# A second layer in seven products of half the width, for the last wide chunk of the second MLP

## The chip, the core and the metric

The kernel runs on one NeuronCore of a Trainium2 chip. The metric is device time in microseconds (us) of one execution; a smaller one is better. TensorE (PE in the profile) multiplies, with weight loads (PEld) beside it; VectorE (DVE), ScalarE (ACT) and GpSimd (POOL) work element by element; DMA transfers are issued from the queue of SyncE (SP). TensorE writes to PSUM, which VectorE and ScalarE read and GpSimd doesn't; everything else lies in SBUF.

## The reference

Four sequences of 576 tokens pass through windowed attention with 8 heads of 64, then through two MLP blocks. What the change touches is the last of them:

```python
def _moe2_ref(x, g_ln, w_ch1, w_ch2):
    mu = np.mean(x, axis=-1, keepdims=True)
    var = np.mean((x - mu) ** 2, axis=-1, keepdims=True)
    xn = (x - mu) / np.sqrt(var + 1e-06) * g_ln
    ch = np.maximum(xn @ w_ch1, 0.0) @ w_ch2
    return (x + ch).astype(np.float32)
```

`x` has 2304 rows (tokens) of 512, `w_ch1` is 512x2048 and `w_ch2` 2048x512. The first MLP block is of the same form with 1536 features.

## The kernel before

The 2304 tokens are 18 tiles of 128; the residual stream is 18 buffers `u[i]` of 128x512. Each operand of a product in the MLPs is split into a rounded high part and a low remainder (`xh`, `xl`, `w1h`, `w1l`, `hh`, `hl`, `w2h`, `w2l`), and a product is three matmuls: high by high, high by low, low by high. The high part is an ACT copy (L361) or a ReLU (L924), the low one a subtraction on DVE or POOL (L374, or L926 for the ReLU).

An MLP runs over three chunks of tokens: a wide one of 8 tiles (0 to 7), a small one of 2 (16, 17), a wide one of 8 (8 to 15). A chunk runs in steps; a step takes 256 features, of which the second MLP has eight. In a wide chunk the first layer of a step (`seven_products`, L977) already is Strassen's scheme in Winograd's form: sums of four quadrants of the tokens' inputs (`prep_wide`) and sums of weights (`w1_of`, tiles `st`) make seven products of 512 columns, six matmuls each, in place of eight. It leaves four blocks `hid[j, half]`: features `j` (0, 1) of 128, tokens of the first or last four tiles (`half`). A block is a ReLU on ACT (`hh`) and one on DVE that subtracts `hh` (`hl`). `keep` holds two PSUM banks into which sums are copied and accumulated upon.

The second layer (`second`, L1036) isn't in that scheme. For each of the 8 token tiles it runs six matmuls of 512 columns (2 feature blocks by 3) into one of two PSUM banks `acc`, whose lines are

```python
nc.tensor.matmul(o.t, hh.t[:, c:c + P], wh.t, start=j == 0, stop=False)
nc.tensor.matmul(o.t, hh.t[:, c:c + P], wl.t, start=False, stop=False)
nc.tensor.matmul(o.t, hl.t[:, c:c + P], wh.t, start=False, stop=j == 1)
```

(L1048 to L1050), and DVE adds the bank to `u[i]` (L1053). In the last step of the last MLP each `u[i]` then goes out by DMA. So a step of a wide chunk has 42 matmuls in the first layer and 48 in the second, all of 512 columns. `w2_of` makes and splits the two tiles of `w_ch2` in the first chunk, stores both parts to DRAM and loads them back in the later chunks.

The second layer of step s stands in the program between the parts of the first layer of step s + 1 (two, three and three tiles after each part). That order isn't the one in which it runs: `Plan` collects every operation with its buffers, gives each a due time from the TensorE work ahead of it, and sets the order of all engines by a list schedule with costs per engine. An operation that names several engines goes to the one that the plan finds best. Buffers are rings with fixed counts: `st`, which takes temporaries of 128x512, has six; `acc` two; `hh` and `hl` six each. A buffer of a ring is used again when every reader of its tenant is done, a DMA store among them.

## Time and profile before

| | |
|---|---|
| median of three runs | 854.18 us (853.12 to 854.47) |
| span of the profiled execution | 854.5 us |
| PE busy | 830.8 us, 97% of the span |
| DVE busy | 638.1 us, 75% |
| ACT, POOL busy | 394.3 us, 338.5 us |

The profiled execution's only own time is its span, which lies 0.3 us over the median of the runs. Sums below are made against the span. The attention fills about the first 170 us, the first MLP reaches to about 480 us, the second MLP's first wide chunk to about 620 us, its small one to about 675 us, and its last wide chunk to the end. TensorE's granted clock is 1.00 (2.4 GHz) in every stretch of 20 us from 200 to 840 us.

### The profile page before, as it was taken

The page shows a single profiled execution, that of the slowest core. Times are in us where ns is not written, and L with a number is a line of the kernel's source. Part 1 is how long each engine was busy: PE and PEld are TensorE (multiplying, and loading weights), DVE is VectorE, ACT ScalarE, POOL GpSimd, SP SyncE. Part 2 cuts the span into 40 slices and gives each one's busy share as a digit, 9 for nine tenths or more (in the row PEclk, how much of TensorE's full clock was granted, in tenths as well). Part 3 has the DMA queues.
Part 4 walks back from the last instruction along what each step waited for, and adds up shares of the span by engine and source line. Part 5 has one row for each costly group of instructions (what it writes and reads, how often), then busy time and mean ns, then how long its engine had stood idle before and what let it go on. Part 6 is the DMA issues. An engine that isn't in the chain of part 4 may idle for free.

```text
span 854.5 us, 13205 instructions
## 1 busy us (share of the span) xinstructions
PE 830.8 (97%) x4478; PEld 685.8 (80%) x4478; DVE 638.1 (75%) x1311; ACT 394.3 (46%) x952; POOL 338.5 (40%) x353
## 2 busy tenths in 40 slices
PE   7999999979999999999999999999999999999997
PEld 6777888758888887788887888788889888888885
DVE  5787777987887989987888956988676855555554
ACT  6888766643434535334357323336357422222220
POOL 2685445554433556532235524614234612221110
PEclk9999999999999999999999999999999999999999
DMA  8678736457677699978762521887477762221112
GB/s 296 187 207 265 242 103 213 146 179 241 200 234 240 228 324 337 348 252 268 264 210 74 178 92 48 264 263 258 154 259 234 247 198 74 74 75 49 50 50 98
DMA packets 73698, 164.96 MB, mean 193 GB/s; under 512 B 8352, under 2 KB 8480, under 8 KB 73632
## 3 DMA queue, kind: packets, MB, share of 16 engines
q1 hardware_dynamic: 73152, 162.83, 57.5%
q0 software_dynamic: 480, 1.31, 0.7%
q8 instruction: 35, 0.57, 0.3%
q14 instruction: 31, 0.25, 0.1%
HBM read 131.34 MB, written 31.46 MB: 191 GB/s over the span
## 4 chain that ended last, share of the span: by engine, by line
PE 83%; DVE 7%; ACT 4%; DMA 2%; issue 2%; POOL 1%; SPq 1%; ACTq 0%; DVEq 0%; POOLq 0%
PE acc L1048 12%; PE acc L1050 12%; PE acc L1049 12%; PE b L993 9%; PE b L995 9%; PE b L994 9%; PE ps_v L608 3%; PE ps_s L596 3%; PE p L848 1%; PE b L442 1%; PE b L441 1%; PE b L440 1%; PE ps_t L653 1%; DVE st L374 1%; PE tok L735 1%
## 5 line engine op out<-in xcount | busy, mean ns | idle before, releaser
L1053 DVE TENSOR_TENSOR u<-acc,u 128x512 f32<-128x512 f32 x252 | 172.9, 687 | 64.0 <-PE acc L1050 60.6
L1048 PE MATMUL acc<-w2h,hh 128*128 128x512 f32 x504 | 198.6, 394 | 5.3 <-DVE u L1053 4.7
L1050 PE MATMUL acc<-w2h,hl 128*128 128x512 f32 x504 | 196.6, 390 | 0.3 <-DVE hl L926 0.2
L1049 PE MATMUL acc<-w2l,hh 128*128 128x512 f32 x504 | 196.5, 390 | 0.0
L924 ACT ACTIVATE hh<-b 128x512 fp32r<-128x512 f32 (+1 forms) x140 | 74.5, 552 | 262.8 <-PE b L995 226.4
L993 PE MATMUL b<-xh,w1h 128*128 128x512 f32 x392 | 154.0, 393 | 3.6 <-DVE hl L926 3.4
L994 PE MATMUL b<-xl,w1h 128*128 128x512 f32 x392 | 153.3, 391 | 1.8 <-DVE xl L374 1.8
L995 PE MATMUL b<-xh,w1l 128*128 128x512 f32 x392 | 153.4, 391 | 0.2 <-DVE w1l L374 0.2
L926 DVE SCALAR_TENSOR_TENSOR hl<-b,hh 128x512 fp32r<-128x512 f32 (+1 forms) x140 | 85.8, 631 | 62.9 <-ACT hh L924 62.1
L374 POOL TENSOR_TENSOR w1l<-w,w1h 128x512 fp32r<-128x512 f32 (+1 forms) x53 | 67.6, 1275 | 134.0 <-ACT w1h L361 124.2
L1048 PEld LDWEIGHTS acc<-w2h,hh 128*128 128x128 f32 x504 | 94.7, 188 | 27.0 <-DVE u L1053 7.5
L1050 PEld LDWEIGHTS acc<-w2h,hl 128*128 128x128 f32 x504 | 94.6, 188 | 21.2 <-DVE hl L926 1.2
L1049 PEld LDWEIGHTS acc<-w2l,hh 128*128 128x128 f32 x504 | 94.7, 188 | 18.4
L374 POOL TENSOR_TENSOR w1l<-st,w1h 128x512 fp32r<-128x512 f32 x38 | 51.1, 1346 | 116.5 <-ACT w1h L361 103.2
L993 PEld LDWEIGHTS b<-xh,w1h 128*128 128x128 f32 x392 | 73.9, 189 | 19.8 <-DVE hl L926 3.8
L994 PEld LDWEIGHTS b<-xl,w1h 128*128 128x128 f32 x392 | 74.0, 189 | 17.4 <-DVE xl L374 2.3
L995 PEld LDWEIGHTS b<-xh,w1l 128*128 128x128 f32 x392 | 73.9, 189 | 16.1 <-DVE w1l L374 0.6
L416 ACT ACTIVATE e<-rh 128x512 bf16<-128x512 bf16 (+2 forms) x65 | 41.3, 635 | 74.0 <-DMA rh<-wb 33.6
L646 ACT ACTIVATE pr<-t,mn 128x128 f32<-128x128 f32 x144 | 55.9, 392 | 15.1 <-DVE mn L637 14.9
L663 POOL TENSOR_SCALAR_AFFINE_SELECT pf<-pf 128x512 f32<-128x512 f32 x64 | 42.3, 661 | 37.7 <-ACT pf L361 35.5
L374 DVE TENSOR_TENSOR b<-b,p 128x512 f32<-128x512 f32 x56 | 39.0, 697 | 23.6 <-PE b L995 23.1
L374 POOL TENSOR_TENSOR w2l<-w,w2h 128x512 fp32r<-128x512 f32 x23 | 32.1, 1395 | 46.1 <-ACT w2h L361 46.0
(118 smaller groups left out, 1369.3 us busy)
## 6 DMA issues: line engine op xcount, KB each, us to landing
w<-d SPq DMA_DIRECT2D x88, 256.0 KB, 4.6
rw<-wb SPq DMA_DIRECT2D x32, 512.0 KB, 4.5
rh<-wb SPq DMA_DIRECT2D x32, 512.0 KB, 4.7
rw<-wa SPq DMA_DIRECT2D x24, 512.0 KB, 4.5
rh<-wa SPq DMA_DIRECT2D x24, 512.0 KB, 4.5
d<-y SPq DMA_DIRECT2D x32, 256.0 KB, 4.4
keys<-kT SPq DMA_DIRECT2D x18, 256.0 KB, 4.3
q<-qT SPq DMA_DIRECT2D x18, 256.0 KB, 4.7
```

The source lines that it names most:

```text
L374: pl.op({e: cost[e] for e in on}, lambda e: ENGINE[e].tensor_tensor(get(), ga(), gb(), alu), [*several(a), *several(b), *also], several(dst))
L646: op({"ACT": 580}, lambda m=m: nc.scalar.activation(out=pr.t[:, m], in_=t.t[:, m], func=AF.Exp, bias=mn.t[:, m:m + 1], scale=-1.0, accum_o ...
L663: op({"POOL": 630}, lambda a=a: nc.gpsimd.affine_select(pf.t[:, a], pf.t[:, 1], [[0, 4], [1 - 2 * a, P]], (ALU.is_ge, ALU.is_gt)[a], 0.0, ...
L924: op({"ACT": act(n, True)}, lambda: nc.scalar.activation(out=hh.t[:, c], in_=go(), func=AF.Relu), [o], [(hh, key)])
L926: mark[0] = op({"DVE": dve(n)}, lambda: nc.vector.scalar_tensor_tensor(out=hl.t[:, c], in0=go(), scalar=0.0, in1=hh.t[:, c].bitcast(F32), ...
L993: nc.tensor.matmul(g.t, wh.t[:, w], xh.t, start=start and k == 0, stop=False, skip_group_check=True)
L994: nc.tensor.matmul(g.t, wh.t[:, w], xl.t, start=False, stop=False, skip_group_check=True)
L995: nc.tensor.matmul(g.t, wl.t[:, w], xh.t, start=False, stop=stop and k == 1, skip_group_check=True)
L1048: nc.tensor.matmul(o.t, hh.t[:, c:c + P], wh.t, start=j == 0, stop=False)
L1049: nc.tensor.matmul(o.t, hh.t[:, c:c + P], wl.t, start=False, stop=False)
L1050: nc.tensor.matmul(o.t, hl.t[:, c:c + P], wh.t, start=False, stop=j == 1)
L1053: op({"DVE": dve(DM)}, lambda o=o, i=i: nc.vector.tensor_tensor(u[i].t, o.t, u[i].t, ALU.add), [o], [u[i]])
```

## The change

In the last wide chunk of the second MLP (`FAST2`), the second layer too is done in seven products. The blocks are 2 feature blocks by 2 halves of the tokens by 2 halves of the output columns; a group `g` takes two tiles of each half, and there are two groups. A product is six matmuls of 256 columns, two tiles by three, so a step has 2 x 7 x 6 = 84 of them in place of 48 of 512.

- **Sums of features** (`parts_of`): `s1` to `s4`, made from the ReLU blocks by DVE, which takes one ReLU and one addition in one instruction (`relu_with`); blocks 00 and 11 are written a second time, unsplit, by ACT. `s1` to `s4` are then split, the high part on ACT, the low one on DVE or POOL.
- **Sums of weights** (`keep_sums`): made in the first wide chunk from the two tiles of `w_ch2`, four sums `t1` to `t4` of 128x256 in two `st` tiles, split with two more `st` tiles, and stored to DRAM (four DMAs of 256 KB per step). `sums_of` loads them in the last chunk (512 KB of high parts and 512 KB of low ones per step) into buffers that the conversion of weights used before.
- **Adding up** (`second_fast`): a group's banks are `a` and `c` (ring `acc`, two) and `b`, into which ACT copies `a` (`fork`) and on which matmuls then accumulate. Six additions of DVE per group go to `u`, each from a bank of two tiles by 256 columns, in place of four of 128x512. `TURNS` is the order in the program.
- The residual is one tile `u_all`, of which `u[i]` are slices, so that one addition reaches two tiles.
- `pe2` is the cost by which the plan counts a matmul of the new form.

```diff
+FAST2 = ((1, 2),)
+
+TURNS = [(0, 0), (1, 0), (2, 0), (5, 0), (3, 0), (0, 1), (6, 0), (1, 1), (4, 0), (2, 1), (5, 1), (3, 1), (6, 1), (4, 1)]
...
+def pe2(n):
+    return 13 + n / 2.4
...
-    u = [buf("big", [P, DM], F32, f"u{i}") for i in range(NTILE)]
+    u_all = buf("big", [P, NTILE, DM], F32, "u")
+    u = [Part(u_all, lambda t, i=i: t[:, i]) for i in range(NTILE)]
...
+        if any((layer, k) in FAST2 for k in range(c + 1, 3)) and c == 0:
+            keep_sums(layer, n, wtiles[used[0] - 2:used[0]], last)
+        return out if (layer, c) not in FAST2 else sums_of(layer, n, out)
+
+    def keep_sums(layer, n, w, last):
+
+        x0, x1 = w
+        temp = [buf("mlp", [P, DM], F32, "st", ST_BUFS) for _ in range(2)]
...
+        sub(0, x0, half(x0, 1), x0, half(x0, 0))
+        sub(1, x1, half(x1, 1), (temp[0], 0), t[0])
+        sub(2, x0, half(x0, 1), x1, half(x1, 1))
+        sub(3, x1, half(x1, 0), (temp[0], 1), t[1])
+        for k, y in enumerate(temp):
...
+            copy(h, lambda h=h: h.t.bitcast(F32R), y, lambda y=y: y.t, DM, ("ACT",))
+            minus(y, lambda y=y: y.t.bitcast(F32R), y, lambda y=y: y.t, h, lambda h=h: h.t, DM)
+            for p, z in (("h", h), ("l", y)):
+                op({"DMA": 728}, lambda k=k, p=p, z=z: nc.sync.dma_start(
+                    out=d[p].t[:, k * DM:(k + 1) * DM], in_=z.t), [z], [(d[p], k)], last)
...
+    def sums_of(layer, n, parts):
+
+        d = sums2[layer, n]
+        hi = buf("raw", [P, 2 * DM], F32R, "rw", 2)
...
+                op({"DMA": 1456 / len(xs)}, lambda p=p, k=k, x=x, w=w: nc.sync.dma_start(
+                    out=x.t.bitcast(F32), in_=d[p].t[:, k * w:(k + 1) * w]), [d[p]], [x])
...
+            if fast:
+                return parts_of(hid, j, half, g)
...
+    def parts_of(hid, j, half, g):
...
+        def split_h(x, h, k=None):
+            (hh, ghh), (hl, ghl) = inner(x, h, k)
+            t = temps[x]
+            split(hh, ghh, hl, ghl, t, lambda: t.t, CW, ("ACT",))
...
+        def relu_both(x, temporary):
+            h = hh, hl = hidden()
+            inner(x, h)
+            op({"ACT": act(CW, True)}, lambda: nc.scalar.activation(out=hh.t, in_=g.t, func=AF.Relu), [g], [hh])
...
+                op({"ACT": act(CW, True)}, lambda: nc.scalar.activation(out=t.t, in_=g.t, func=AF.Relu), [g], [t])
+            mark[0] = op({"DVE": dve(CW)}, lambda: nc.vector.scalar_tensor_tensor(
+                out=hl.t, in0=g.t, scalar=0.0, in1=hh.t.bitcast(F32), op0=ALU.max, op1=ALU.subtract), [g, hh], [hl])
...
+        def relu_with(x, y, alu):
+            t, z = temp(x), temps[y]
+            op({"DVE": dve(CW)}, lambda: nc.vector.scalar_tensor_tensor(
+                out=t.t, in0=g.t, scalar=0.0, in1=z.t, op0=ALU.max, op1=alu), [g, z], [t])
+            return t
+        if j == half:
+            relu_both("11" if j else "00", True)
+        elif half:
+            h = few()
+            s1 = relu_with("s1", "11", ALU.add)
+            relu_with("s3", "00", ALU.subtract)
+            s2, a = temp("s2"), temps["00"]
+            minus(s2, lambda: s2.t, s1, lambda: s1.t, a, lambda: a.t, CW)
+            split_h("s1", h, 0)
+            split_h("s3", h, 1)
+            split_h("s2", hidden())
+        else:
+            relu_both("01", False)
+            relu_with("s4", "s2", ALU.subtract)
+            split_h("s4", hidden())
...
+    def second_fast(s, w2, hid):
...
+        def bank_of(group, x):
+            if x not in group[3]:
+                group[3][x] = buf("psn", [P, 2, HW], F32, "acc", 2)
+            return group[3][x]
+
+        def product(group, x, h, w, start, stop):
...
+                for p in range(2):
+                    c = slice((2 * g + p) * P, (2 * g + p + 1) * P)
+                    for k, (x, y) in enumerate(((ghh, gwh), (ghh, gwl), (ghl, gwh))):
+                        nc.tensor.matmul(o.t[:, p], x()[:, c], y(), start=start and p == 0 and k == 0,
+                                         stop=stop and p == 1 and k == 2, skip_group_check=True)
...
+        def fork(group):
+            tag = f"p{group[2]}"
+            a, b = group[3]["a"], buf("psm", [P, 2, HW], F32, tag)
+            group[3]["b"] = b
...
+                    b.t.rearrange("p a b -> p (a b)"), x.t[:, :P], x.t, start=True, stop=False, skip_group_check=True), [x], [b])
+            op({"ACT": act(CW, True)}, lambda: nc.scalar.activation(out=b.t, in_=a.t, func=AF.Copy), [a], [b])
...
+        def add(group, x, other, half):
+            o, i = group[3][x], group[1] if other else group[0]
+            c = slice(half * HW, (half + 1) * HW)
+            op({"DVE": dve(CW)}, lambda: nc.vector.tensor_tensor(
+                u_all.t[:, i:i + 2, c], o.t, u_all.t[:, i:i + 2, c], ALU.add), [o, u[i], u[i + 1]], [u[i], u[i + 1]])
...
+        for k, g in TURNS:
+            group = groups[g]
+            if k == 0:
+                product(group, "a", "00", "00", True, False)
+                fork(group)
+            elif k == 1:
+                product(group, "c", "s1", "t1", True, False)
+                add(group, "c", True, 1)
+            elif k == 2:
+                product(group, "b", "s2", "t2", False, False)
+                add(group, "b", False, 1)
+            elif k == 3:
+                product(group, "b", "s3", "t3", False, False)
+                add(group, "b", True, 1)
+            elif k == 4:
+                product(group, "b", "11", "t4", False, True)
+                add(group, "b", True, 0)
+                done(group, True)
+            elif k == 5:
+                product(group, "a", "01", "10", False, True)
+                add(group, "a", False, 0)
+            else:
+                product(group, "c", "s4", "11", False, True)
+                add(group, "c", False, 1)
+                done(group, False)
...
-        units = second(*before) if before else iter(())
+        units = iter(())
+        if before:
+            units = (second_fast if steps[before[0]][:2] in FAST2 else second)(*before)
...
-            parts, ns = seven_products(w1, xs, keep, s == len(steps) - 1, hid), (2, 3, 3, 0)
+            parts = seven_products(w1, xs, keep, s == len(steps) - 1, hid, (layer, c) in FAST2)
+            ns = (6, 8, 0, 0) if before and steps[before[0]][:2] in FAST2 else (2, 3, 3, 0)
```

How the instructions move, word for word, at three places; the engines and queues on which an instruction waits stand in brackets behind it. DVE, one step of the last chunk: `u` is the residual, `acc`, `p0` and `p1` are the banks `a` or `c`, `b` of group 0 and `b` of group 1; `hl` and `hh` are parts of the hidden blocks, `b0` to `b3` the first layer's banks, `w1l` a part of a weight. Before:

```order
L1053 TENSOR_TENSOR u12_1651<-acc_9095,u12_1651 128x512 [waits PE_49]
L1053 TENSOR_TENSOR u13_1755<-acc_9103,u13_1755 128x512 [waits PE_49]
L926 SCALAR_TENSOR_TENSOR hl_9129<-b0_9005,hh_9125 128x512 [waits Activation_49]
L1053 TENSOR_TENSOR u14_1900<-acc_9118,u14_1900 128x512 [waits PE_49]
L374 TENSOR_TENSOR w1l_9151<-st_8782,w1h_9138 128x512 [waits Activation_49]
L1053 TENSOR_TENSOR u15_2028<-acc_9131,u15_2028 128x512 [waits PE_49]
L926 SCALAR_TENSOR_TENSOR hl_9165<-b2_9024,hh_9143 128x512 [waits Activation_49]
L926 SCALAR_TENSOR_TENSOR hl_9188<-b3_2498,hh_9184 128x512 [waits Activation_49]
L926 SCALAR_TENSOR_TENSOR hl_9192<-b1_2301,hh_9186 128x512 [waits DVE_49,Activation_49]
```

After, from the sum `s1` (`st_9653`) on, with `s3` (`st_9661`) and `s4` (`st_9708`):

```order
L1130 SCALAR_TENSOR_TENSOR st_9653<-b3_2481,st_9640 128x512 [waits PE_49,Activation_49,Pool_49]
L1130 SCALAR_TENSOR_TENSOR st_9661<-b3_2481,st_9611 128x512 [waits Pool_49]
L1231 TENSOR_TENSOR u_324<-p0_9503,u_324 128x2x256 [waits DVE_49,PE_49]
L1231 TENSOR_TENSOR u_324<-p1_9590,u_324 128x2x256 [waits DVE_49,PE_49]
L1231 TENSOR_TENSOR u_324<-acc_9576,u_324 128x2x256 [waits PE_49]
L1125 SCALAR_TENSOR_TENSOR hl_9691<-b2_9557,hh_9645 128x512 [waits Activation_49]
L1231 TENSOR_TENSOR u_324<-p0_9503,u_324 128x2x256 [waits PE_49]
L1130 SCALAR_TENSOR_TENSOR st_9708<-b1_2284,st_9663 128x512 [waits Pool_49]
L395 TENSOR_TENSOR st_9725<-w_9099,w_9122 128x256 [waits DMAHW3_49,DMAHW2_49,DVE_49]
L1231 TENSOR_TENSOR u_324<-p1_9590,u_324 128x2x256 [waits PE_49]
L395 TENSOR_TENSOR st_9714<-st_9714,w_9099 128x256 [waits Pool_49]
L1125 SCALAR_TENSOR_TENSOR hl_9743<-b1_2284,hh_9723 128x512 [waits Activation_49]
```

In place of one addition per tile there are additions of pairs of half tiles, three per bank `p0` or `p1`, between which the bank is multiplied into again; the sums of features stand among them.

PE, just behind the last product of the last first layer, the end of the program. Before, tile by tile, two banks in turn:

```order
L1048 MATMUL acc_9315<-w2h_9153,hh_9278 128x512 [waits DMAHW0_49,DVE_49,Activation_49]
L1049 MATMUL acc_9315<-w2l_9156,hh_9278 128x512 [waits DMAHW1_49]
L1050 MATMUL acc_9315<-w2h_9153,hl_9282 128x512
L1048 MATMUL acc_9315<-w2h_9167,hh_9309 128x512 [waits DMAHW2_49,Activation_49]
L1049 MATMUL acc_9315<-w2l_9169,hh_9309 128x512 [waits DMAHW3_49]
L1050 MATMUL acc_9315<-w2h_9167,hl_9313 128x512 [waits DVE_49]
L1048 MATMUL acc_9322<-w2h_9153,hh_9278 128x512
```

After, the last product of group 1 of the step before (`acc_9845`, its last row), then the first one with the sum `s1` (`fewh`) of the last step:

```order
L1212 MATMUL acc_9845<-w2l_9541,hh_9741 128x256
L1212 MATMUL acc_9845<-w2h_9528,hl_9758 128x256
L1212 MATMUL acc_9945<-rw_9712,fewh_9886 128x256 [waits DMAHW4_49,DVE_49,Activation_49]
L1212 MATMUL acc_9945<-y_9642,fewh_9886 128x256 [waits DMAHW3_49]
L1212 MATMUL acc_9945<-rw_9712,fewl_9895 128x256 [waits Pool_49]
L1212 MATMUL acc_9945<-rw_9712,fewh_9886 128x256
L1212 MATMUL acc_9945<-y_9642,fewh_9886 128x256
L1212 MATMUL acc_9945<-rw_9712,fewl_9895 128x256
L1212 MATMUL p0_9936<-rw_9712,hh_9925 128x256 [waits Activation_49]
```

The product into `acc_9945` now waits for the addition (DVE) that frees the bank of `acc_9845`, and for a split of `s1` (ACT).

POOL in the first wide chunk of the second MLP. `st` are sums of weights, `w` tiles of weights, `w1l` and `w2l` low parts. Before:

```order
L374 TENSOR_TENSOR st_5831<-w_5782 128x256 [waits DMAHW6_49]
L374 TENSOR_TENSOR w1l_5843<-w_5180,w1h_5819 128x512 [waits PE_49,Activation_49]
L374 TENSOR_TENSOR st_5831<-st_5831,w_5752 128x256 [waits DMAHW5_49,Pool_49]
L374 TENSOR_TENSOR st_5857<-w_5752,st_5831 128x256 [waits Pool_49]
L374 TENSOR_TENSOR w1l_5891<-st_5735,w1h_5877 128x512 [waits PE_49,Activation_49]
L374 TENSOR_TENSOR w1l_5907<-w_5226,w1h_5896 128x256 [waits PE_49,Activation_49]
```

After:

```order
L395 TENSOR_TENSOR st_5928<-w_5735,st_5855 128x256 [waits DMAHW1_49,Pool_49]
L395 TENSOR_TENSOR st_5972<-w_5840 128x256 [waits DMAHW7_49,DMAHW2_49,DVE_49]
L395 TENSOR_TENSOR st_5972<-w_5940,st_5972 128x256 [waits DMAHW3_49,Pool_49]
L395 TENSOR_TENSOR w2l_6003<-w_5940,w2h_5988 128x512 [waits DMAHW4_49,Activation_49]
L395 TENSOR_TENSOR st_5972<-st_5972,st_6005 128x512 [waits DVE_49,Activation_49]
L395 TENSOR_TENSOR w1l_6059<-w_5735,w1h_6046 128x512 [waits PE_49,Activation_49]
L395 TENSOR_TENSOR st_6075<-w_5993 128x256 [waits DMAHW5_49,DMAHW2_49,Pool_49]
L395 TENSOR_TENSOR st_6075<-st_6075,w_5986 128x256 [waits DMAHW1_49,Pool_49]
L395 TENSOR_TENSOR w1l_6112<-st_5928,w1h_6106 128x512 [waits PE_49,Activation_49]
L395 TENSOR_TENSOR st_6129<-w_5986,st_6075 128x256 [waits DMAHW4_49,DMAHW6_49,DVE_49,Pool_49]
L395 TENSOR_TENSOR w2l_6143<-w_6073,w2h_6127 128x512 [waits DMAHW7_49,DMAHW4_49,Activation_49]
```

Between the first layer's sums (`st_5928`, `st_6075`, `st_6129`) now stand sums of the second layer's weights (`st_5972`, three rows), and sums of the next step wait for DMAs, among which are the stores that empty their `st` buffers.

## Rows read from the trace of the kernel before

**Rows 1.** The page's head and part 1: engine, busy us (share of the span), instructions.

```profile
span 854.5 us, 13205 instructions
...
PE 830.8 (97%) x4478; PEld 685.8 (80%) x4478; DVE 638.1 (75%) x1311; ACT 394.3 (46%) x952; POOL 338.5 (40%) x353
```

**Rows 2.** Windows of 20 us: length, busy PE, PEld, DVE, ACT, POOL, clock, DMA share, GB/s.

```profile
520.00:540.00 20.00, 19.19 (x85) 15.57 (x84) 15.46 (x23) 7.52 (x14) 12.23 (x10) 1.00 0.27 82
540.00:560.00 20.00, 20.00 (x90) 16.53 (x89) 18.61 (x30) 6.64 (x13) 9.62 (x9) 1.00 0.84 288
560.00:580.00 20.00, 20.00 (x90) 16.57 (x89) 16.75 (x28) 6.40 (x13) 4.71 (x4) 1.00 0.79 261
720.00:740.00 20.00, 20.00 (x90) 16.57 (x89) 11.03 (x17) 4.72 (x10) 4.42 (x5) 1.00 0.24 79
```

**Rows 3.** Timeline, ACT, last chunk: start, length; the same block in two steps.

```profile
730.61 0.60 ACT L924 ACTIVATE hh<-b 128x512 fp32r<-128x512 f32 x1 [10.69 <-PE b L995]
...
751.01 0.60 ACT L924 ACTIVATE hh<-b 128x512 fp32r<-128x512 f32 x1 [10.69 <-PE b L995]
```

**Rows 4.** Timeline, PE, small chunk: first and last of 19 matmuls in a row.

```profile
648.08 0.28 PE L442 MATMUL b<-fewh,w1l 128*128 128x256 f32 x1
...
650.23 0.28 PE L442 MATMUL b<-fewh,w1l 128*128 128x256 f32 x1
```

**Rows 5.** Groups by shape, 610 to 700 us: weight loads of those matmuls, busy us, mean ns.

```profile
L442 PEld LDWEIGHTS b<-fewh,w1l 128*128 128x128 f32 x64 | 12.2, 191 | 0.0
```

**Rows 6.** Groups by shape, 694 to 855 us: busy us, mean ns, idle before, its releaser.

```profile
L1053 DVE TENSOR_TENSOR u<-acc,u 128x512 f32<-128x512 f32 x66 | 45.5, 690 | 26.9 <-PE acc L1050 25.8
...
L926 DVE SCALAR_TENSOR_TENSOR hl<-b,hh 128x512 fp32r<-128x512 f32 x30 | 19.9, 685 | 32.2 <-ACT hh L924 32.2
...
L924 ACT ACTIVATE hh<-b 128x512 fp32r<-128x512 f32 x30 | 16.9, 596 | 114.7 <-PE b L995 114.7
...
L374 POOL TENSOR_TENSOR w1l<-st,w1h 128x512 fp32r<-128x512 f32 x7 | 9.0, 1291 | 44.6 <-ACT w1h L361 44.6
L361 ACT ACTIVATE w1h<-st 128x512 fp32r<-128x512 f32 x13 | 8.2, 629 | 0.0
...
L374 POOL TENSOR_TENSOR st<-w 128x256 f32<-128x256 f32 x4 | 2.9, 734 | 13.0 <-DMA w<-d 9.6 <-issue 3.4
...
L374 DVE TENSOR_TENSOR st<-w 128x256 f32<-128x256 f32 x4 | 1.7, 415 | 0.0
```

**Rows 7.** DVE on low parts of sums, whole span: ns least, median, most; first, last start.

```profile
L374 DVE TENSOR_TENSOR w1l<-st,w1h x18: 674/1076/1080, 175.4 to 814.2; 128x512 fp32r<-128x512 f32 x18
```

**Rows 8.** Waits of PE, 300 to 500 us: us in total, times, longest.

```profile
PE acc L1048 <- DVE u L1053: 3.9, 4, 1.9
```

**Rows 9.** Waits of PE, 500 to 700 us.

```profile
PE acc L1048 <- DVE u L1053: 0.8, 1, 0.8
```

**Rows 10.** Timeline, PE, end of the last first layer and start of the last second layer.

```profile
837.62 0.39 PE L995 MATMUL b<-xh,w1l 128*128 128x512 f32 x1
...
839.24 0.50 PE L1048 MATMUL acc<-w2h,hh 128*128 128x512 f32 x1 [0.56 <-ACT hh L924]
...
840.08 0.50 PE L1050 MATMUL acc<-w2h,hl 128*128 128x512 f32 x1
```

**Rows 11.** Timeline, ACT and DVE, there: the last two blocks' high and low parts.

```profile
838.11 1.08 ACT L924 ACTIVATE hh<-b 128x512 fp32r<-128x512 f32 x2 [4.41 <-PE b L995]
...
838.74 1.29 DVE L926 SCALAR_TENSOR_TENSOR hl<-b,hh 128x512 fp32r<-128x512 f32 x2 [2.72 <-ACT hh L924]
```

**Rows 12.** Timeline, DVE: the last addition before the end.

```profile
850.16 0.69 DVE L1053 TENSOR_TENSOR u<-acc,u 128x512 f32<-128x512 f32 x1 [0.67 <-PE acc L1050]
```

**Rows 13.** DMA issues from 838 us on: count, KB each, median us from issue to landing.

```profile
out<-u SPq DMA_DIRECT2D x8, 256.0 KB, 2.0
```

More of the change, by code (lines that the diff above doesn't have):

```diff
@@ L100, in t, with __init__ @@
         return self.tile
+class Part(Buf):
+    def __init__(self, whole, get):
+        self.plan, self.pool, self.spec = whole.plan, whole.pool, whole.spec
+        self.ops, self.track, self.after, self.behind, self.first = [], {}, [], None, set()
+        self.whole, self.get = whole, get
+    @property
+    def t(self):
+        return self.get(self.whole.t)
 class Plan:
@@ L974, in w2_of, with half, sub @@
             out.append(x)
-        return out
-    def seven_products(ws, xs, keep, end, hid):
+        if any((layer, k) in FAST2 for k in range(c + 1, 3)) and c == 0:
[4 more added lines that the diff above has]
+        temp = [buf("mlp", [P, DM], F32, "st", ST_BUFS) for _ in range(2)]
+        d = {p: buf("dram", [P, 2 * DM], F32, f"ds{layer}{n}{p}") for p in "hl"}
+        t = [(lambda c=c: temp[c // 2].t[:, c % 2 * HW:(c % 2 + 1) * HW]) for c in range(4)]
+        def half(x, c):
+            return lambda: x.t[:, c * HW:(c + 1) * HW]
+        def sub(c, a, ga, b, gb):
+            minus((temp[c // 2], c % 2), t[c], a, ga, b, gb, HW)
+        sub(0, x0, half(x0, 1), x0, half(x0, 0))
[3 more added lines that the diff above has]
+        for k, y in enumerate(temp):
+            h = buf("mlp", [P, DM], F32, "st", ST_BUFS)
+            copy(h, lambda h=h: h.t.bitcast(F32R), y, lambda y=y: y.t, DM, ("ACT",))
[3 more added lines that the diff above has]
+                    out=d[p].t[:, k * DM:(k + 1) * DM], in_=z.t), [z], [(d[p], k)], last)
+        sums2[layer, n] = d
```

51 lines of the change are left out of this document (49 added, 2 removed).

## The prediction

> **What bounds the kernel now.** First the page's head and first part: PE is busy for 830.8 of 854.5 us, no other engine for more than 75% [rows 1]. Then windows of 20 us, to see the stages apart. In the last wide chunk PE is busy for 20.00 of 20.00 us at a granted clock of 1.00, beside DVE with 11.03, ACT with 4.72 and POOL with 4.42; in the second MLP's first wide chunk PE is as full, but DVE has 15.5 to 18.6 [rows 2]. Where PE waits there, it is for DVE's addition that frees an `acc` bank: once for 0.8 us from 500 to 700 us [rows 9], four times for 3.9 us from 300 to 500 us [rows 8]. So time is PE's matmuls, and what an edit takes from PE is gained as long as DVE keeps up.
>
> A matmul's price is the distance from start to start, not its busy time, since matmuls overlap. The same ReLU block comes 20.40 us later in the next step [rows 3]; with 42 + 48 matmuls in a step that is 226.7 ns for 512 columns. For 256 columns the small chunk has a run of 19 starts in 2.15 us, 18 distances of 119.4 ns [rows 4]: the same operands' types, another weight for each. A weight load there lasts 191 ns [rows 5], longer than the distance, so loads overlap and don't set it. Half the columns thus cost 53%, not 50%.
>
> **The change part by part, against the span of 854.5 us.**
>
> *PE.* A product of 6 matmuls of 256 columns takes 6 x 0.1194 = 0.717 us, a second layer 14 of them = 10.03 us in place of 48 x 0.2267 = 10.88. I count up to the end of the last first layer, since the end is another matter. Before it stand seven second layers, 336 matmuls, 76.2 us. After the change three products of the seventh have slipped behind it, so 95 are left, 68.1 us; two matmuls of 512 columns that set up the banks `b` add 0.45. That is 76.2 - 68.5 = **-7.7 us**.
>
> At 2.4 GHz the columns alone would take 213.3 and 106.7 ns, so the rows lie 13.4 and 12.7 ns above them. The Trainium skill, TensorE: Matmul & The Clock Gate, section Back-to-back issue gap, gives N/2.4 + 2.5 ns for a matmul on a warm clock, which would be 109.2 ns for 256 columns. The distances of this trace don't agree with it for either width; with its 109.2 and the measured 226.7 the term would be -13.5 us.
>
> *Other engines in a step of the last chunk,* of 19.5 us now. DVE gets 12 additions for 8, 3 blocks `hl` for 4, the sums `s1`, `s3`, `s4`, and as before two additions of first-layer banks: 20 x 0.69, and with two half sums of 0.42 and a low part of 1.08 that is 15.7 us [rows 6, 7], 80%. POOL: seven low parts or sums of 1.29 and three of 0.73, 11.3 us. ACT: seven more of 0.6, 8.9 us. All fit. An addition of two runs of 256 isn't in the trace; its bounds are two of 0.42 and one of 0.69, and I take 0.69, which it equals in elements and in its PSUM source.
>
> Whether they come in time I followed through one step by the order: a first-layer product 6 x 0.2267 = 1.36 us, results 0.16 us after the next may start (0.39 - 0.23, [rows 10]), each engine in its order. The nearest wait is at product `c` of group 0. Its bank is freed by the addition of `c` of group 1 of the step before, and on DVE ahead of that stand, from 19.0 us after the step's start on, an addition (to 19.7), `s4` (20.4), a half sum (20.8), an addition (21.5), a half sum (22.0), `hl` of block 01 (22.6) and the addition itself (23.3); PE is there at 23.8. That leaves 0.5 us; `hl` of 01 leaves 0.6 us, and the low part of 1.08 behind them 0.5. No wait, then, but the slack is less than one addition. Seven steps at nothing up to 0.5 us: I take **+0.3**, near nothing, as in the busier first chunk PE waits once in 200 us [rows 9]; bound 3.5.
>
> *The end.* Before: the last first-layer matmul starts at 837.62, the next could at 837.85. PE then waits for the last ReLU block, high part (838.11 on ACT) and low part (838.74 on DVE), goes on at 839.24 and 840.08 [rows 10, 11], and the last addition ends at 850.16 + 0.69 = 850.85 [rows 12]: 13.0 us. After, with 0 where PE is free: three products of the step before and product `a` end at 2.9. DVE meanwhile is a queue: `s3` and `s2` to 1.3, additions and `s4` to 4.0, the last of which frees the bank for `c` of group 0. PE waits for it from 2.9 to 4.1. Behind it on DVE stand three low parts (to 6.5), then the addition of that `c`, to 7.2, for which the next product into it waits. From there PE and DVE take turns: additions end at 7.9, 8.6, 9.3, 10.0, 11.1, 11.8, 12.6, 13.3, 14.0, 14.7. The last product accumulates on the bank that the second last was added from, so it waits until 14.7, ends at 15.8, and its addition at 16.4. With the SBUF-only operations at 0.67, the low end of [rows 7], it is 15.9; I take 16.2, **+3.2** (2.6 to 3.7). So over a third of PE's gain goes back, since 17 products need 12.2 us but DVE's additions between them don't overlap.
>
> *Last DMAs.* Two tiles go out at once in place of one. One takes 2.0 us from issue to landing [rows 13]; 288 GB/s at a share of 0.84 [rows 2] make 343 at 1.0, 0.76 us for 256 KB. **+0.7**, between 0 and 2.0.
>
> *Sums of weights, first wide chunk.* Per step four half sums, two high parts and two low parts, on ACT 2 x 0.63, on DVE or POOL 4 x 0.42 or 0.73 and 2 x 1.08 or 1.29 [rows 6, 7]: counted in the order with these durations, seven steps have some 7 us more on DVE and 24 on POOL beside 142 us of PE. DVE there goes from 84% to 89%; PE's own work doesn't change. The cover is DVE's rest; where it is full, PE waits 0.8 to 1.9 us at a time [rows 8, 9]. I take one more such wait, **+0.8**, between 0 and 3.9, which 200 us of the fuller first MLP lose. Loads of the sums (1 MB per step) meet a chunk at a DMA share of 0.24 and are issued a step ahead: nothing.
>
> *The residual as one tile* costs nothing: waits in the attention and the first MLP are those of before.
>
> Sum: -7.7 + 0.3 + 3.2 + 0.7 + 0.8 = -2.7, span 851.8; the median lies 0.3 under the span: **851.5**.
>
> **Rivals.** *(1) DVE sets the pace of the last chunk.* For: 80% busy, slack of 0.5 us, and each engine runs in order, so one late operation delays all behind it. Against: a wait lets DVE catch up, and DVE held 93% at 540 to 560 us beside a full PE [rows 2]. Price: 7 x 0.5 = 3.5 in place of 0.3: 854.7, no change.
>
> *(2) Slower: the ring of six `st` buffers in the first wide chunk.* A step now takes four more of them, held until their stores have landed, and the next step's first-layer sums, in order on POOL and DVE, wait for that. If it costs PE one wait of 0.8 [rows 9] in each of eight steps, it is 6.4 in place of 0.8: 857.1. It decides from 0.65 us a step on, where the sum passes +1.7. For: some of these sums do wait for stores in the order. Against: they are made a step ahead of their products, 20 us, so a late store has to hold up something else in the queue.
>
> *(3) The new matmuls take their columns' time alone.* If what the rows have above it, 13 ns, doesn't fall on products of 256 columns in the last chunk, 570 matmuls take 60.8 us, PE's term is -14.9 in place of -7.7, and the time 844.3. For it: the run of [rows 4] is from another chunk. Against it: it has the same types, a new weight for each matmul, and the last chunk's own 512 columns have the same 13 ns [rows 3]. The rule of the Trainium skill's TensorE page named above is nearly this case; by it the time would be 845.7.
>
> **How the numbers follow.** The forecast has a chance of 0.61, from 849.1 (its extras at their low ends: -7.7 + 2.6 = -5.1) to 853.6; rival 1 has 0.20, rival 2 0.17, rival 3 0.02. Faster or slower by more than 0.2%, 1.7 us, is about what a measurement of this kernel can tell from no change: the bounds are 852.5 and 855.9. Of the forecast 0.53 lies under the first, with rival 3 that is 0.55; between them lie 0.08 of it, all of rival 1 and 0.03 of rival 2, 0.31; slower 0.14. The range for 8 in 10 runs from 849.0 to 856.0: it takes in rival 1 and leaves out most of rival 2 and rival 3.
>
> **What would show it.** In the profile after: 119 to 120 ns between starts of the new matmuls; 19.5 to 19.6 us from a ReLU block to the same one in the next step (20 or more: rival 1); PE waiting for DVE about 3 us in all behind the last first-layer product; the last addition some 16 us behind it; waits of PE from 480 to 620 us at 1 to 2 us in all (5 or more: rival 2). Additions of 128x2x256 far off 0.69 would move the end and the slack at once.

## The result, and the profile after

The changed kernel takes 860.99 us (median of seven executions; the kernel before 854.89 in the same series): a ratio of 1.0075, 95% interval 1.0055 to 1.0095. One of the seven took 1027 us at a mean granted clock of 0.75; the ratio leaves it out. A second series gave 860.22 us and 1.0066 (1.0045 to 1.0087). It is slower by some 6 us; forecast were 851.5 us, at most 856.0, and faster.

The head and part 1 of its page, to be read beside [rows 1]:

```profile
span 859.0 us, 14151 instructions
...
PE 829.3 (97%) x4768; PEld 693.8 (81%) x4768; DVE 696.0 (81%) x1383; ACT 437.0 (51%) x1024; POOL 413.3 (48%) x417
```

DVE is busy for 58 us more. The waits of PE from 480 us to the end (us in total, times, longest); before, this list had one wait for DVE, of 0.8 us, and one for ACT, of 0.6:

```profile
PE acc L1177 <- DVE hl L948: 3.1, 2, 2.4
PE acc L1175 <- DVE u L1180: 1.8, 2, 1.3
PE acc L1212 <- ACT p L1226: 0.8, 1, 0.8
PE p L1212 <- DVE u L1231: 0.8, 1, 0.8
PE b L1065 <- DVE b L395: 0.5, 1, 0.5
```

The 20 us windows of the second MLP's first wide chunk and one of the last, with the columns of [rows 2]:

```profile
540.00:560.00 20.00, 18.68 (x83) 15.14 (x82) 19.82 (x29) 5.95 (x11) 13.35 (x13) 1.00 0.79 254
560.00:580.00 20.00, 19.94 (x87) 15.88 (x86) 18.71 (x29) 8.09 (x15) 10.70 (x10) 1.00 0.88 287
580.00:600.00 20.00, 17.57 (x78) 14.19 (x77) 18.78 (x26) 9.12 (x17) 14.58 (x13) 1.00 0.83 300
...
800.00:820.00 20.00, 20.00 (x127) 17.77 (x126) 15.13 (x24) 9.11 (x17) 10.97 (x11) 1.00 0.34 119
```

The loss shows in the first wide chunk, where PE was full or nearly so before. The last chunk looks full, and here the busy time misleads. From start to start a step there takes 20.11 us (timeline of ACT, the same copy in two steps), not the 19.5 forecast:

```profile
745.14 0.58 ACT L382 ACTIVATE b<-b 128x512 f32<-128x512 f32 x1
...
765.25 0.58 ACT L382 ACTIVATE b<-b 128x512 f32<-128x512 f32 x1
```

A wait shorter than a matmul's modelled length leaves no gap in PE's busy time. So for the rest I use a measure of my own, **PE's excess**: from the timeline of PE each distance between the starts of two matmuls, less 226.7 ns (512 columns) or 119.4 ns (256), added up. Some 5 us of each sum are 60 matmuls of 128 columns, the same in both kernels, for which the measure has no price.

| excess, us | 440–480 | 480–620 | 620–680 | 680 to the end | sum |
|---|---|---|---|---|---|
| before | 5.5 | 1.9 | 3.3 | 1.2 | 11.9 |
| after | 5.5 | 6.8 | 4.8 | 5.6 | 22.7 |

PE's work falls by 6.4 us (eight second layers, 384 x 226.7 ns = 87.05, against 672 x 119.4 ns and two of 226.7 = 80.69). The excess rises by 10.8. That leaves +4.4, and the spans differ by 4.5.

### The profile page after: what moved, and what is told of

Its sections match the earlier page's. It is cut to its first block, busy times and chain, and to the rows that moved or that the text cites. A ratio compares the mean times of both kernels' runs of the same rounds, so it can differ in the third digit from the quotient of the medians.

```text
span 859.0 us, 14151 instructions
## 1 busy us (share of the span) xinstructions
PE 829.3 (97%) x4768; PEld 693.8 (81%) x4768; DVE 696.0 (81%) x1383; ACT 437.0 (51%) x1024; POOL 413.3 (48%) x417
## 3 DMA queue, kind: packets, MB, share of 16 engines
q0 software_dynamic: 480, 1.31, 0.7%
## 4 chain that ended last, share of the span: by engine, by line
PE 79%; DVE 10%; ACT 4%; issue 3%; DMA 2%; POOL 1%; SPq 0%; DVEq 0%; POOLq 0%; ACTq 0%
PE b L1065 9%; PE b L1067 9%; PE b L1066 9%; PE acc L1175 8%; PE acc L1177 8%; PE acc L1176 8%; PE acc L1212 5%; PE p L1212 4%; PE ps_v L629 3%; PE ps_s L617 2%; DVE st L395 2%; PE p L870 1%; PE ps_t L674 1%; PE b L463 1%; PE b L462 1%
## 5 line engine op out<-in xcount | busy, mean ns | idle before, releaser
L1180 DVE TENSOR_TENSOR u<-acc,u 128x512 f32<-128x512 f32 x188 | 128.5, 685 | 38.0 <-PE acc L1177 36.7
L1175 PE MATMUL acc<-w2h,hh 128*128 128x512 f32 x376 | 148.8, 396 | 5.7 <-DVE u L1180 5.6
L1177 PE MATMUL acc<-w2h,hl 128*128 128x512 f32 x376 | 147.0, 391 | 3.3 <-DVE hl L948 3.3
L1176 PE MATMUL acc<-w2l,hh 128*128 128x512 f32 x376 | 146.8, 390 | 0.0
L946 ACT ACTIVATE hh<-b 128x512 fp32r<-128x512 f32 (+1 forms) x108 | 56.3, 541 | 124.0 <-PE b L1067 90.6
L1175 PEld LDWEIGHTS acc<-w2h,hh 128*128 128x128 f32 x376 | 70.7, 188 | 23.3 <-DVE u L1180 9.9
L1177 PEld LDWEIGHTS acc<-w2h,hl 128*128 128x128 f32 x376 | 70.6, 188 | 19.9 <-DVE hl L948 4.9
L948 DVE SCALAR_TENSOR_TENSOR hl<-b,hh 128x512 fp32r<-128x512 f32 (+1 forms) x108 | 64.4, 614 | 21.2 <-ACT hh L946 20.3
L1176 PEld LDWEIGHTS acc<-w2l,hh 128*128 128x128 f32 x376 | 70.7, 188 | 13.3
L395 POOL TENSOR_TENSOR st<-w 128x256 f32<-128x256 f32 x50 | 42.5, 859 | 30.8 <-DVE w L452 14.3
```

Source lines behind the costliest of these rows:

```text
L395: pl.op({e: cost[e] for e in on}, lambda e: ENGINE[e].tensor_tensor(get(), ga(), gb(), alu), [*several(a), *several(b), *also], several(dst))
L946: op({"ACT": act(n, True)}, lambda: nc.scalar.activation(out=hh.t[:, c], in_=go(), func=AF.Relu), [o], [(hh, key)])
L948: mark[0] = op({"DVE": dve(n)}, lambda: nc.vector.scalar_tensor_tensor(out=hl.t[:, c], in0=go(), scalar=0.0, in1=hh.t[:, c].bitcast(F32), ...
L1180: op({"DVE": dve(DM)}, lambda o=o, i=i: nc.vector.tensor_tensor(u[i].t, o.t, u[i].t, ALU.add), [o], [u[i]])
```

## What holds DVE up

The second longest wait behind 480 us in the changed kernel, for the addition that frees `acc`, with all that DVE and POOL did before it (merged timeline, 547 to 553 us; start, length):

```profile
547.75 1.29 POOL L395 TENSOR_TENSOR w1l<-st,w1h 128x512 fp32r<-128x512 f32 x1 [1.71 <-ACT w1h L382]
547.90 1.42 DVE L444 TENSOR_SCALAR m<-rw 128x512 uint32<-128x512 uint32 x1
549.12 0.81 POOL L395 TENSOR_TENSOR st<-w 128x256 f32<-128x256 f32 x1
549.25 0.84 DVE L440 TENSOR_SCALAR s<-e 128x256 int32<-128x256 int32 x1
549.89 0.77 POOL L395 TENSOR_TENSOR w1l<-w,w1h 128x256 fp32r<-128x256 f32 x1
550.12 0.84 DVE L442 SCALAR_TENSOR_TENSOR s<-e,s 128x256 int32<-128x256 int32 x1
550.63 1.22 POOL L497 TENSOR_TENSOR w<-y,g_sb 128x512 f32<-128x512 f32 x1
550.88 1.26 DVE L395 TENSOR_TENSOR st<-w,st 128x256 f32<-128x256 f32 x1
552.06 0.68 DVE L1180 TENSOR_TENSOR u<-acc,u 128x512 f32<-128x512 f32 x1
...
552.79 0.50 PE L1175 MATMUL acc<-w2h,hh 128*128 128x512 f32 x1 [1.32 <-DVE u L1180]
```

Each of the four DVE instructions before the addition ends 0.15 to 0.3 us after the POOL instruction beside it (549.32 after 549.04; 552.14 after 551.85). Alone they take 0.41, 0.28, 0.41 and 0.41 us. They were waiting inside their busy time, for POOL. This is no chance of the place: from 480 to 620 us, in both kernels, each of the 42 instructions with two SBUF operands that lasted over 0.06 us longer than alone ends 0.28 us (128x256) or 0.55 us (128x512) behind the POOL instruction that was running when it began, 0.13 us less than its own time. Sorted over 480 to 620 us by whether a POOL instruction was running when they began (mean length in us, count):

| DVE instruction | before, alone | before, beside a POOL subtraction | after, beside one | `pool_writes` (below), beside a POOL fill |
|---|---|---|---|---|
| a PSUM operand, 128x512 | 0.69 (56) | 0.69 (23) | 0.68 (31) | 0.69 (25) |
| two SBUF operands, 128x256 | 0.42 (15) | 1.10 (4) | 1.05 (16) | 0.41 (7) |
| two SBUF operands, 128x512 | 0.68 (12) | 1.05 (9) | 1.19 (15) | 0.68 (8) |
| shift of one operand, 128x512 | 0.41 (fastest) | 1.36 (4) | 1.08 (8) | 0.52 (8) |

Summing what each contending instruction took over its time alone gives DVE's **held time**, 480 to 620 us: 14.4 us before (21 of 62 instructions held up), 27.2 after (42 of 76). Their own work went from 29.7 to 36.7: the 7 us more that the prediction counted are there, and 12.8 of waiting with them. The Trainium skill, SBUF — State Buffer, section Who interferes with whom, has the rule: a DVE instruction with two SBUF inputs contends with a GpSimd instruction that reads SBUF, one in a two-port mode with GpSimd whatever it does, and the second one waits until the first is done. The trace agrees, with the rows of this table, down to the exception for an operand in PSUM.

## Experiments

*Theory 1*: this port. *Theory 2*: DVE simply has too many instructions. *Theory 3*: the ring of `st`, my rival 2. A ring of its own for the sums has no run: it needs 50 KB of each partition, and 44 are left.

### Which half of the change costs

`sums_only` makes and stores the sums and never loads them; the last chunk is that of before.

```diff
-        return out if (layer, c) not in FAST2 else sums_of(layer, n, out)
+        return out
...
-            units = (second_fast if steps[before[0]][:2] in FAST2 else second)(*before)
+            units = second(*before)
...
```

> The sums of weights are made, split and stored in the first wide chunk as in the changed kernel, and never loaded: the last wide chunk has the second layer of before. What the sums cost is seen alone. In the changed kernel the distances from matmul to matmul in excess of 226.7 and 119.4 ns add up to 6.8 us from 480 to 620 us against 1.9 before, and to 4.8 from 620 to 680 against 3.3. If the sums are the cause: about 861 (854.9 + 6.4). If it is a chance of the new order that the last chunk's change brought: 855. The prediction's own term, +0.8: 855.7.

861.94 us, 1.0078 (1.0053 to 1.0104): the whole loss, without the last chunk. Part of it is the clock's. In two windows of its trace PE waits 1.3 us for ACT and 0.2 for DVE (distances 1.5 and 0.4 us too long), and then matmuls of 512 columns start 0.43 us apart in place of 0.23 (the third number from the end is the granted clock, 0.70 on average: 1.2 GHz for part of these 5 us, 2.4 for the rest):

```profile
630.00:635.00 5.00, 3.97 (x31) 3.49 (x30) 2.73 (x5) 5.00 (x13) 1.32 (x2) 1.00 0.76 253
635.00:640.00 5.00, 4.46 (x15) 3.44 (x16) 3.19 (x7) 2.47 (x7) 1.45 (x2) 0.70 0.93 281
```

The same follows the wait at 465 us, which the kernel before has too, there without a fall of the clock. Together this is some 3 us of this trace.

`fast_only` makes the sums for the first step alone (`and n == 0`) and loads these in every step.

> The sums of weights are made and stored for the first step alone, and the last wide chunk loads these eight times: the output is not the reference's. The last chunk's work is that of the changed kernel, the first wide chunk's nearly that of before. If the loss is in the sums alone: 852 to 853 (matmuls -6.4, waits in the last chunk +2.2, the end +2.2). If the last chunk loses by itself: 855 or more.

854.13 us, 0.9987 (0.9972 to 1.0001). The new second layer gains some 1 us when its sums are free, and by the interval between nothing and 2.4: its excess behind 680 us is 5.6 us, as in the full change, against 1.2. So both halves miss the forecast: the sums by some 6 us, the last chunk by some 2.

### Why the sums cost

`sums_pool` puts the six subtractions of a step on POOL alone, `on=("POOL",)`.

> The changed kernel, with the six subtractions of the sums on GpSimd alone, so VectorE has the instructions of before from 480 to 620 us. Theory 1, a shared port (VectorE's instructions with two SBUF operands last longer while GpSimd works): VectorE's busy time from 480 to 620 us stays 8 us or more above the 108 of before though it has nothing more to do, and PE's excess there stays at 4 to 8 us: 859 to 862. Theory 2, VectorE has too many instructions: busy time back to 108 to 111, excess 2 to 3 us: 856. Theory 3, the ring of st: as the changed kernel, 860, with VectorE's times those of before.

858.11 us, 1.0028 (1.0015 to 1.0041). The stretch of 480 to 620 us in the kernel before (columns of [rows 2]), then in the changed one:

```profile
480.00:620.00 140.00, 139.19 (x619) 115.00 (x618) 107.99 (x177) 54.68 (x109) 53.72 (x47) 1.00 0.56 188
...
480.00:620.00 140.00, 135.23 (x589) 109.68 (x588) 122.39 (x188) 56.35 (x109) 77.46 (x71) 1.00 0.71 246
```

and in `sums_pool`:

```profile
480.00:620.00 140.00, 136.50 (x596) 111.00 (x595) 117.56 (x176) 55.92 (x109) 88.48 (x82) 1.00 0.72 249
```

DVE has 176 instructions in place of 177 and is busy 9.6 us longer; 25.4 us of it are held time. PE's excess there is 5.3. Theory 2 can't give that. The time, though, lies below the 859 to 862 that theory 1 was to give, some 2 us under the changed kernel's: DVE's own instructions can have a part.

`pool_reads` and `pool_writes` are the kernel **before**, with nothing added but POOL work in the same steps: eight subtractions from the two weight tiles, or 20 fills, into a tile that nobody reads.

```diff
...
+        for _ in range(8):
+            op({"POOL": pool_tt(HW)}, lambda: nc.gpsimd.tensor_tensor(
+                even.t, ws[0].t[:, :HW], ws[1].t[:, :HW], ALU.subtract), ws, [even])
...
```

```diff
...
+        for _ in range(20):
+            op({"POOL": 300}, lambda: nc.gpsimd.memset(even.t, 0.0), ws, [even])
...
```

> The kernel before, in whose first wide chunk of the second MLP GpSimd does eight subtractions of 128x256 more in a step, from the two weight tiles into a tile that nobody reads: some 42 us more of GpSimd from 480 to 620 us, and nothing more for any other engine, no buffer of st, no DMA. Theory 1 (shared port): VectorE's busy time there goes from 108 to 116 us or more with the same instructions, the mean of 128x512 with two SBUF operands from 0.75 up, and PE's excess from 1.9 to 4 us or more: 857 to 861. Theory 2 (VectorE has too many instructions) and theory 3 (ring of st): nothing changes, 855.

> The same, with 20 fills of 128x256 a step in place of the eight subtractions: about as much GpSimd time, but nothing that it reads from SBUF. If the port is taken by GpSimd's reads: VectorE's busy time near 108 to 111 us, PE's excess 2 us, 855. If anything that GpSimd does holds VectorE up, or the weight tiles that come free late are the cause: as the kernel with subtractions.

With reads 860.70 us, 1.0072 (1.0048 to 1.0097); with fills 853.88, 0.9985 (0.9971 to 1.0). The same stretch with reads:

```profile
480.00:620.00 140.00, 136.98 (x600) 112.24 (x599) 114.01 (x181) 54.15 (x108) 80.80 (x82) 0.99 0.52 177
```

and with fills:

```profile
480.00:620.00 140.00, 138.21 (x611) 114.08 (x610) 110.78 (x186) 55.64 (x112) 77.62 (x151) 0.99 0.52 177
```

POOL is busy for 80.8 and 77.6 us. With reads the kernel takes 5.7 us more, with fills none: held time 19.6 against 12.8, excess from 440 us to the end 18.9 against 12.1 (11.9 before). Neither has a new tile of `st`, a DMA or work for ACT. The planner did move a few low parts from POOL to DVE in both (181 and 186 instructions for 177), which is part of DVE's 114.0 (116 or more were expected) but the same in the control. This is theory 1, reproduced in a kernel without the change.

The sign of this pair is surer than its size, since the planner's order differs between the two. From 480 to 620 us alone the excess is 6.3 with reads and 5.4 with fills (1.9 before); the rest of the difference lies from 440 to 480 us, with 8.0 against 3.1 (5.5 before). The control's longest wait behind 440 us,

```profile
PE acc L1052 <- DVE u L1057: 1.8, 1, 1.8
```

ends at 526 us behind two DVE instructions of 1.31 and 1.75 us that began beside POOL's own subtractions, not beside fills.

`sums_dve` puts the six subtractions on DVE alone.

> The changed kernel with the six subtractions of the sums on VectorE alone: GpSimd has no more to do in the first wide chunk than before, VectorE some 3.0 us more in each of eight steps. Theory 1 (port) alone: VectorE's other instructions last as long as before, its busy time from 480 to 620 us is 108 + 21 = 129 of 140 us, and PE's excess from 440 us on falls from 22.7 to 18 or 19: 856. Theory 2 (VectorE is full): the excess stays at 22 or more: 860.

859.53 us, 1.0061 (1.0043 to 1.0079); DVE has 215 instructions and 124.2 us busy, 18.8 of them held time, and the excess from 440 us on is 25.1. Theory 1 alone would have given 856. So theory 2 holds on this side: what the port no longer takes, the instructions do. The sums fit on neither engine.

`no_stores` drops the stores but for the first step; `other_stores` keeps them but takes their bytes from the weights' parts, so that `st` comes free at once.

> The changed kernel with the sums made and split in every step, but stored in the first step alone and those loaded eight times (the output is not the reference's): st tiles come free as soon as the arithmetic on them is done, and 7 MB of stores are gone. Theory 3 (ring of st, or the stores' traffic): PE's excess from 480 to 620 us falls from 6.8 to 2 us, 855 to 856. Theories 1 and 2: it stays at 5 us or more, 859 to 861.

> The changed kernel whose four stores a step take the parts of the second-layer weights in place of the sums' parts (same bytes, same queue; the output is not the reference's). The sums are made and split as before, but their st tiles come free when the arithmetic is done. Leaving the stores out altogether gave 856.5 against 860.5. If the ring of st made that difference: 856 to 857 again. If the traffic did: 860 to 861.

856.53 us, 1.0029 (1.0012 to 1.0046), and 859.30, 1.0048 (1.0027 to 1.0069). The ring's part is then 1 us or so, within the interval. The stores' absence took 4 us off the median, but in the trace the excess fell only from 22.7 to 22.1 and held time from 27.2 to 25.4. That execution took 860.06 us, the second longest of ten, so its trace doesn't show what the median lost: where these 4 us were, and what part the stores' traffic has, stays open.

### The last chunk

The excess of each step there, 0.5 to 0.6 us, sits at three places: 0.12 us at the product that needs `hl` of block 01, 0.12 at the one into the `acc` bank that an addition behind that `hl` frees, and 0.26 at the next first-layer product. The third in the merged timeline of the changed kernel (PEld is the weight load; POOL's subtraction ends at 766.63, DVE's low part 0.55 us later, and the weight load has waited for it):

```profile
765.34 1.29 POOL L395 TENSOR_TENSOR hl<-st,hh 128x512 fp32r<-128x512 f32 x1
...
765.68 1.50 DVE L395 TENSOR_TENSOR w1l<-st,w1h 128x512 fp32r<-128x512 f32 x1
...
767.23 0.19 PEld L1067 LDWEIGHTS b<-xh,w1l 128*128 128x128 f32 x1 [0.42 <-DVE w1l L395]
767.24 0.50 PE L1067 MATMUL b<-xh,w1l 128*128 128x512 f32 x1
```

Ahead of `hl` of block 01, too, a half sum that lasts 1.50 us stands in DVE's queue, held up in the same way. `last_pool` puts the weights' sums and low parts of the last chunk's first layer on POOL alone.

> The changed kernel with the weights' sums and low parts of the last chunk's first layer on GpSimd alone, so that VectorE has three instructions with two SBUF operands fewer in a step (two half sums and a low part) and GpSimd has 2.8 us more. In the changed kernel PE loses 0.55 us in each step there, at the low part of a ReLU block and at the low part of the weights' sums, both late on VectorE. Theory 1: these go away, a step takes 19.6 us in place of 20.1, and the time falls by 2 to 3.5 us. If GpSimd (then 14 of 20 us) is late instead, a step takes 20 us or more, and the time is the same.

856.81 us, 1.0027 (1.0012 to 1.0041). From 740 to 800 us the excess falls from 1.6 to 0.3: these waits come of the instructions that were moved. Whether of the time that they were held or of their own 1.5 us a step, the edit doesn't tell, since it takes both off DVE. But PE now waits at three other places for 0.7 to 1.3 us, for DVE, for ACT and for a low part of POOL, and behind 680 us the excess is 5.9, not less than 5.6. The time is some 3.5 us lower than the changed kernel's, but in the profiled executions this isn't the edit's: one and the same run of eight transposes in the first MLP starts at 412.20 us here and at 415.88 in the changed kernel, whose second execution has it at 411.74.

`after_again` is the changed kernel a second time.

> The changed kernel once more, on the chip of the runs beside it. If its spread of 856 to 865 us is its own: again about 861. If it came of the first runs: 857 to 859. PE's excess from 440 us to the end 22 to 23 us, as in its first trace (before 11.9), whatever the time.

860.22 us; the excess from 440 us to the end is 25.0 in place of 22.7. Of these 2 us 1.4 are seven matmuls 0.43 us apart (1.2 GHz) from 465 us on, behind a wait that the first execution has too, without a fall of the clock. So between two executions of one kernel it varies by 2 us, and smaller differences of it say nothing.

### A planner that knows the port

`Plan` counts 0.42 us for a half sum whatever POOL does. `lock_before` and `lock_after` are the kernels before and after with one rule more in the list schedule: everything on POOL, and on DVE the subtractions and conversions whose operands all lie in SBUF (`self.port`), don't overlap by more than 0.1 us; an engine takes other work meanwhile.

```diff
+                if (e == "POOL" or e == "DVE" and k in self.port) and self.port_free > at + 100:
+                    later = self.port_free
+                else:
+                    later = sooner(k, e, at) if len(ops[k][0]) > 1 else None
...
+                if e == "POOL" or e == "DVE" and k in self.port:
+                    self.port_free = free[e]
```

> The same planner for the kernel before. Its excess from 440 us on is 11.9 us, 9 of which lie outside the last wide chunk: if the port's order makes them, up to 4 us less: 851 to 854. If they are transitions between chunks, which no order helps: 855.

> The changed kernel whose planner knows the port: subtractions and conversions with SBUF operands alone on VectorE, and everything on GpSimd, never overlap in the list schedule; an engine takes other work meanwhile. The order changes in the whole kernel. If the loss is a matter of order, because the planner counts 0.42 to 0.68 us for what lasts 0.8 to 1.7: excess from 440 us on down by 5 us or more from 22.7, 853 to 856. If VectorE and GpSimd together have too much for the port: 857 to 861.

> The planner that knows the port, with the new second layer in the last chunk and the sums of weights made for the first step alone (the output is not the reference's). The same planner with the kernel before gives 845.1. Under the old planner this edit took 1.0 us off. If the waits of 0.5 us a step in the last chunk come from the port: 845.1 - 6.4 + 2.4 at the end = 841. If they stay (0.4 us a step, as in lock_after): 843 to 844. If the last chunk gains nothing: 845.

> The planner that knows the port, with the sums made and stored and the old second layer everywhere. If the sums cost only because of a bad order: 846 to 847. If VectorE, GpSimd and their port have too much to do in the first wide chunk, whatever the order: 850 to 852.

| time, us | old planner | planner with the port |
|---|---|---|
| kernel before | 854.95 | **845.13**, 0.9887 (0.9872 to 0.9902) |
| sums alone | 861.94 | 849.33 |
| last chunk alone | 854.13 | 844.84 |
| whole change | 860.22 | 850.87, 0.9953 (0.9933 to 0.9974) |

The rows come of several series, in which the kernel before takes 854.95 to 855.17 us. `lock_after` lies below both its cases, `lock_sums_only` between its two. `lock_before` beats both kernels by 1.1% and more. Part 1 of its page:

```profile
PE 828.3 (98%) x4478; PEld 686.0 (81%) x4478; DVE 600.7 (71%) x1318; ACT 392.8 (47%) x952; POOL 326.9 (39%) x346
```

With nearly the same instructions DVE is busy for 37 us less than in [rows 1]. Held time falls from 6.7 to 1.4 us between 160 and 200 us, from 28.8 to 9.9 between 200 and 480, and from 14.4 to 4.5 between 480 and 620. The largest gain is not where I expected it. In the first step of the first MLP the kernel before has these waits of PE (160 to 200 us):

```profile
PE b L993 <- DVE hl L926: 3.4, 1, 3.4
PE b L994 <- DVE xl L374: 1.8, 1, 1.8
```

and `lock_before` one of 0.9 us; from the first copy `b<-b` on ACT to the next are 16.0 us there, 24.2 before. Behind the wait of 3.4 us seven matmuls start 0.43 us apart (1.2 GHz), in `lock_before` none. My expectation for it, 851 to 854, was drawn from the excess behind 440 us alone, which hardly moved (11.9 both times).

The change stays slower by 5.7 us under the new planner, and the last chunk alone gains 0.3, which is nothing clear of noise. The sums cost 4.2 us even in this order: in `lock_after` the held time is 16.9 us from 480 to 620, against 4.5, and the excess 6.3, against 1.6. In the last chunk 0.4 us a step remain, now for `hl` of block 01 (timeline of `lock_after`):

```profile
754.44 0.19 PEld L1223 LDWEIGHTS acc<-w2h,hl 128*128 128x128 f32 x1 [0.16 <-DVE hl L1136]
```

That `hl` lasts 0.68 us, its plain length, and DVE is at 80%. But the queue ahead of it, without a gap since 750.76 us, has a half sum that POOL holds up:

```profile
751.82 0.75 POOL L403 TENSOR_TENSOR st<-w 128x256 f32<-128x256 f32 x1
...
751.97 0.88 DVE L403 TENSOR_TENSOR st<-w 128x256 f32<-128x256 f32 x1
```

It lasts 0.46 us longer than alone, in this step as in the others from 732 us on, and the weight load waits for 0.16. So the port still has a part here; what the queue alone would cost isn't shown. `lock_last` adds the edit of `last_pool` to `lock_after`.

> The whole change, the planner that knows the port, and in the last chunk the weights' sums and low parts of the first layer on GpSimd alone. lock_after is at 850.9. If VectorE's two-operand instructions still cost 0.4 us a step: 848 to 849. If GpSimd, then later, costs as much: 851.

851.68 us, 0.9955 (0.9938 to 0.9973): nothing gained; its excess behind 680 us is 6.9 us, 1.7 of it in one wait-ridden stretch at 780 to 800.

## Why the prediction was wrong, step by step

| step | predicted, us | measured, us |
|---|---|---|
| matmuls, to the last first layer | -7.7 | -7.7 |
| waits in the last chunk | +0.3 (to 3.5) | +3.3 |
| the end | +3.2 (2.6 to 3.7) | +2.4 |
| last two DMAs | +0.7 (0 to 2.0) | -0.1 |
| sums of weights, first wide chunk | +0.8 (0 to 3.9) | +6.4 |
| residual as one tile | 0 | +0.3 up to 440 us |
| span | -2.7 | +4.5 (the terms add up to 4.6) |

**Matmuls: right.** The distances are 0.12 us within the new products and 0.23 in the first layer (medians, at the 0.01 us of the timeline); the addition of two runs of 256 takes 0.684 us, as taken. Rival 3 is out. The Trainium skill's N/2.4 + 2.5 ns (TensorE: Matmul & The Clock Gate, Back-to-back issue gap), which that section gives for an isolated matmul and not for a stream with a weight load each, doesn't agree with these distances either.

**Sums of weights: the step that failed.** "Some 7 us more on DVE and 24 on POOL ... DVE there goes from 84% to 89%. The cover is DVE's rest." DVE went from 77% to 87% (108.0 and 122.4 of 140 us), twice the rise that was counted. The 24 us on POOL came as counted (53.7 and 77.5 us) and were priced at nothing. But POOL's reads and DVE's two-operand instructions exclude each other, so POOL's work comes out of DVE's rest. The bound of 3.9 came from a stage with the same habits and fell with it. The evidence stood in my own rows: [rows 7] gives 674, 1076 and 1080 ns for one and the same instruction, and I took the median as its price instead of asking what the other 400 ns were. I knew no rival of this kind; rival 2 names the right place and, with 6.4, by luck the very price, for a mechanism to which `other_stores` leaves some 1 us. How the 6.4 us divide between held time, DVE's own instructions and the stores isn't shown: `sums_dve` loses as much without the work on POOL. Rival 2's sign, waits of 5 us or more, couldn't tell the two apart.

**Waits in the last chunk: mis-sized.** I walked through the step with 0.42 for the half sum and 1.08 for the low part; the first half sum and the low part last 1.45 to 1.51 each in most steps. With a slack of 0.5 us, that decides it. Rival 1 had the price (3.5, a step of 20 us or more) and the right chain, "one late operation delays all behind it".

**The end: right in kind, a little high.** The last first-layer matmul and the last addition, each from its engine's timeline:

```profile
839.84 0.39 PE L1067 MATMUL b<-xh,w1l 128*128 128x512 f32 x1
...
854.77 0.69 DVE L1231 TENSOR_TENSOR u<-p,u 128x512 f32<-128x512 f32 x1 [1.06 <-PE p L1212]
```

From 840.07, where PE is free, to 855.46 are 15.4 us against 13.0. PE waits in two places, 0.8 us each (first list above); the alternation of PE and DVE that I forecast came at the last product alone. The two last DMAs cost nothing: 3.5 us from the last addition to the end, 3.65 before.

## What to carry to other kernels

An engine with idle time is free cover only if it shares nothing with the engine that is full: where POOL subtracts in SBUF, DVE's SBUF-only instructions stand still inside their busy time. The sign in a profile is one shape with two lengths (0.41 and 1.1, 674 and 1076 ns) while instructions with a PSUM operand keep theirs; price POOL work by what it adds to those. If a list schedule sets the order, put such a port into it as a resource: here that alone was worth 1.1%, more than the change could have brought.
